# Query halves of the first two tiles ahead of the fused matrices in the head of an attention-branch backward kernel

## The chip, the cores and the metric

The kernel runs on one core of a Trainium2 chip. The metric is the device time of one execution in microseconds, as the median over runs. The engines are named as in the profile: PE is TensorE (PEld its weight loads), DVE is VectorE, ACT is ScalarE, POOL is GpSimd, and SP is SyncE, which only issues DMAs here.

## The reference

One block of a speech encoder is computed forward, then all gradients for a given output gradient. The forward part, cut:

```
xa = layernorm(x)                                  # x: 2 x 4000 x 144
q, k, v = split(xa @ w_qkv)
p = softmax(q @ k^T * 144**-0.5)                   # 4000 x 4000 for each batch
glob = (p @ v) @ w_att_out
h = gelu(layernorm(x) @ w_mlp_in)
u, g = split(h);  g = layernorm(g)
gc = depthwise_conv(g, dw_csgu, 5 taps over time)
loc = (u * gc) @ w_mlp_out
m = concat(glob, loc)
m = m + depthwise_conv(m, dw_merge, 5 taps over time)
out = x + m @ w_merge
```

The kernel returns `out` and the gradients of x and of the seven weights, in bf16.

## The kernel before, in words

The 4000 tokens of a batch are 32 blocks of 125. The two batches are worked off one after the other. For each, `phase_att` runs a loop over tiles t (one tile is one block of 125 queries) with eight steps s in each. A tile's work is spread over three turns of the loop:

- `S_pair(t, s)`, s = 0 to 3: two matmul pairs give 125x1000 scores in PSUM (L740, L741). DVE writes the running negative maximum (L745, L747), ACT the exponentials into `Pbuf` (L748).
- `rescale(t)` after s = 3: the four chunks are put on one maximum (L753, L757, L759), and SP issues the DMA that transposes all of P into `PT` (L760).
- One turn later `Y_half` (L768) multiplies `PT` by the normalized input, and `dP_pair` (L790, L791) makes the gradient of the scores, which DVE combines with P into `Sbuf` (L794). Later still `Z_half` (L810) and `X_group` (L849) use these.

`PT` exists once, and the PSUM pool for the scores and for dP has two buffers, which are handed out in the order of the program. All small products share a PSUM pool of three buffers.

A tile needs a query operand `qt` of two halves. The first half (for S) is the normalized input times the fused matrix `Q0` (and its last 16 rows in `RW`), Wq times Wk transposed. The second half (for dP) is the output gradient times the fused matrices `VUT` (and `RW`), which hold Wv, Wo, the taps of the depthwise convolution and w_merge in one. `jit_mm` (L707 to L714) and `jit_tr` (L722, L724) make both halves at once: a product into PSUM, two copies by ACT, PE transposes, one more copy. `jit_q` (L873 to L877), `jit_b` (L890 to L895) and `half_tr` (L884, L885) make one half each.

The head of the first batch is a program of its own (`head` in the main function). It loads x, the weights and the output gradient, and has these pieces:

- `st`, `mv`, `ln`, `xat` for each of four groups of eight blocks: statistics on DVE (L361 to L372), the power for the inverse deviation on POOL (L373), the factor on DVE (L377), normalizing of each block (L382 on ACT, L384 on DVE, L386 on POOL), PE transposes (L391, L395), and copies into `xaT_m` by ACT (L392) and into `R` by DVE (L396).
- `m1` makes `Q0`, `m1t` its transpose, `cols` the taps as columns, `taps` the products of w_merge with the taps (h = 0 on ACT, L217; h = 1 on POOL, L219), `tapr` their remainders on POOL (L223).
- `vo` makes the transposed weights WT; `vut` makes `VUT` from WT and the tap products (L232 to L239); `vu` makes what the output stage needs, and spills it to DRAM (small products on POOL, L261); `conv` makes the matrices of the local branch (POOL, L280 to L303, with ten tiny column loads).
- `gma`, `gm`, `gmb` transpose the output gradient into `goT` (L349, L350), `gs` its last 16 channels into `R` (L356, L357); `gr` copies these channels on POOL (L399).
- `clear` writes a block of zeros to DRAM (L1420, L1421), and `pads` loads these into the unused rows of `Pbuf` and `Sbuf` (L682, L683).

The order on the engines comes from the framework: it gives each instruction the priority of its place in the program and plans each engine's list ahead of time with its own estimates. An engine named in `manual_schedule` keeps the written order for the instructions traced inside; others may be put between them. Before the change this holds for POOL through the whole head (`k.head_order`) and for DVE in a block that ends ahead of the loop. The rest of the head is dealt out over the list `steps`: entry 8t + s is traced ahead of step s of tile t, for t = 0 and 1. From tile 2 on, `local_units` (the MLP branch) is dealt out over the loop; its tiles reuse the memory of the head's.

Of the kernel before, what the change touches and what calls it, by code (L numbers as in the profile page):

```python
# [14 lines left out]
D = 144  # L15
DR = 16
# [92 lines left out]
class Head:  # L109
# [7 lines left out]
    def loads(self):  # L117

        k, W, nc, wp, wt = self.k, self.W, self.k.nc, self.k.wpool, self.wt
        self.raw = wt.tile([128, 2, 7 * D], BF, name="raw")  # L120
        nc.vector.memset(self.raw[:, 1, :], 0.0)
        make_identity(nc, W.ident[:])
        self.two = wt.tile([128, 7, 2, D], BF, name="two")
        nc.gpsimd.memset(self.two[:, :, 1, :], 0.0)
        W.M1T = wp.tile([128, 2, D], BF, name="M1T")
        nc.gpsimd.memset(W.M1T[:, 1, :], 0.0)
        W.RW = wp.tile([128, 3 * D], BF, name="RW")
        nc.gpsimd.memset(W.RW[:], 0.0)
        W.Wi = wp.tile([128, 2, 2 * D], BF, name="Wi")
        nc.gpsimd.memset(W.Wi[:, 1, :], 0.0)  # L130
        self.Wi2 = wt.tile([DR, 2 * D], BF, name="Wi2")
        W.cols = wp.tile([128, 6, 5], F32, name="cols")
        nc.gpsimd.memset(W.cols[:], 0.0)
        self.dwt = wt.tile([5, 3 * D], BF, name="dwt")
        r = self.raw
        self.Wqkv, self.Wo, self.Wl = r[:, :, 0:3 * D], r[:, :, 3 * D:4 * D], r[:, :, 4 * D:5 * D]
        self.Wm = [r[:, :, (5 + h) * D:(6 + h) * D] for h in range(2)]

        def ld(t, ap, r0, eng=nc.scalar):
            eng.dma_start(t[0:128, 0, :], ap[r0:r0 + 128, :])  # L140
            eng.dma_start(t[0:DR, 1, :], ap[r0 + 128:r0 + D, :])
        ld(self.Wqkv, k.w_qkv, 0)
        ld(self.Wo, k.w_att_out, 0)
        nc.scalar.dma_start(self.dwt[:, 0:2 * D], k.dw_merge)
        nc.scalar.dma_start(self.dwt[:, 2 * D:3 * D], k.dw_csgu)
        ld(self.Wl, k.w_mlp_out, 0)
        for h in range(2):
            ld(self.Wm[h], k.w_merge, h * D, nc.sync)
        nc.scalar.dma_start(W.Wi[0:128, 0, :], k.w_mlp_in[0:128, :])
        nc.scalar.dma_start(W.Wi[96:96 + DR, 1, :], k.w_mlp_in[128:D, :])  # L150
        nc.scalar.dma_start(self.Wi2[:], k.w_mlp_in[128:D, :])

    def transp(self, src, c0, n):
        nc, ident = self.k.nc, self.W.ident
# [182 lines left out]
def pre_pieces(k, W, b, S, pst):  # L337
# [4 lines left out]
    if True:  # L342
        def v8(t, i0, n):
            return t[:, i0 * PB:(i0 + n) * PB].rearrange("p (a b) -> p a b", b=PB)

        def gomain(h0, n):
            pm = pst()
            for bi in range(n):
                nc.tensor.transpose(pm[:, bi, 0:PB], go_q[:, 2 + h0 + bi, 0:128], W.ident[0:PB, 0:PB])  # L349
            nc.scalar.copy(v8(S.goT, h0, n), pm[:, 0:n, 0:PB])  # L350

        def gostack(g):
            pm = pst()
            for bi in range(8):
                j = 8 * g + bi
                nc.tensor.transpose(pm[0:80, bi, 0:PB], S.go_r[:, j + 2:j + 7, :].rearrange("p a b -> p (a b)"), W.ident[0:PB, 0:PB])  # L356
            nc.vector.tensor_copy(v8(S.R, 8 * g, 8)[0:80], pm[0:80, :, 0:PB])  # L357

        def ln_st(g):
            for j in range(8 * g, 8 * g + 8):  # L360
                nc.vector.bn_stats(st[:, j, :], x_tp[:, j, :])  # L361

        def ln_mv(g):

            sl = slice(8 * g, 8 * g + 8)
            ma, mb, va, vb = st[:, sl, 1], st[:, sl, 4], st[:, sl, 2], st[:, sl, 5]
            nc.vector.tensor_tensor(S.dm[:, sl], ma, mb, op=ALU.subtract)
            nc.vector.tensor_tensor(S.sm[:, sl], ma, mb, op=ALU.add)
            nc.vector.tensor_tensor(veps[:, sl], va, vb, op=ALU.add)
            nc.vector.scalar_tensor_tensor(S.dm[:, sl], S.dm[:, sl], 0.25 * D, S.dm[:, sl], op0=ALU.mult, op1=ALU.mult)  # L370
            nc.vector.tensor_tensor(veps[:, sl], veps[:, sl], S.dm[:, sl], op=ALU.add)
            nc.vector.tensor_scalar(veps[:, sl], veps[:, sl], 1.0 / D, EPS, op0=ALU.mult, op1=ALU.add)  # L372
            nc.gpsimd.tensor_tensor(S.rstd_x[:, sl], veps[:, sl], k.mhalf[0:PB, sl], op=ALU.pow)  # L373

        def ln_nm(g):
            sl = slice(8 * g, 8 * g + 8)
            nc.vector.scalar_tensor_tensor(nmr[:, sl], S.sm[:, sl], -0.5, S.rstd_x[:, sl], op0=ALU.mult, op1=ALU.mult)  # L377

        def ln(g):
            for j in range(8 * g, 8 * g + 8):  # L380
                if S.act_ln and j % 2 == 0:
                    nc.scalar.activation(S.xa_aug[:, j, 0:D], x_tp[:, j, :], ACT.Identity, scale=S.rstd_x[:, j:j + 1], bias=nmr[:, j:j + 1])  # L382
                elif S.act_ln or j % 2:
                    nc.vector.tensor_scalar(S.xa_aug[:, j, 0:D], x_tp[:, j, :], S.rstd_x[:, j:j + 1], nmr[:, j:j + 1], op0=ALU.mult, op1=ALU.add)  # L384
                else:
                    nc.gpsimd.tensor_scalar(S.xa_aug[:, j, 0:D], x_tp[:, j, :], S.rstd_x[:, j:j + 1], nmr[:, j:j + 1], op0=ALU.mult, op1=ALU.add)  # L386

        def xat(g):
            pm = pst()
            for bi in range(8):  # L390
                nc.tensor.transpose(pm[:, bi, 0:PB], S.xa_aug[:, 8 * g + bi, 0:128], W.ident[0:PB, 0:PB])  # L391
            nc.scalar.copy(v8(S.xaT_m, 8 * g, 8), pm[:, :, 0:PB])  # L392
            pr = pst()
            for bi in range(8):
                nc.tensor.transpose(pr[0:112, bi, 0:PB], S.xa_aug[:, 8 * g + bi, 32:D], W.ident[0:PB, 0:PB])  # L395
            nc.vector.tensor_copy(v8(S.R, 8 * g, 8)[96:112], pr[96:112, :, 0:PB])  # L396

        def go_rem():
            nc.gpsimd.tensor_copy(S.go_r[:], go_q[:, :, 128:D])  # L399
        P = {}  # L400
        for g in range(G8):
            P["st%d" % g] = lambda g=g: ln_st(g)
            P["mv%d" % g] = lambda g=g: ln_mv(g)
            P["ln%d" % g] = lambda g=g: (ln_nm(g), ln(g))
            P["xat%d" % g] = lambda g=g: xat(g)
            P["gm%d" % g] = lambda g=g: gomain(2 + 8 * g, 8)
            P["gs%d" % g] = lambda g=g: gostack(g)
        P["gma"] = lambda: gomain(0, 2)
        P["gmb"] = lambda: gomain(NB + 2, 2)
        P["gr"] = go_rem  # L410
        return P
# [252 lines left out]
def phase_att(k, W, b, S, A, M, head=None):  # L664
# [6 lines left out]
    with ExitStack() as es:  # L671
# [225 lines left out]
        if head is None:  # L897
            jit_mm(0)
            jit_tr(0)
        else:  # L900
            steps = head(dict(pads=pads, clr=clr, jit_q=lambda: jit_q(0), jit_b=lambda: jit_b(0), jit_1=lambda: (jit_mm(1), jit_tr(1))))
        for t in range(NB + 1):
            xg = X_groups(t)
            if t == NB - 1:
# [7 lines left out]
            for s in range(8):  # L912
# [14 lines left out]
                        zt_tr(t - 3)  # L927
                    x(1)
                elif s == 1:
                    if ok(t + 1) and (t or head is None):  # L930
                        jit_mm(t + 1)
                    x(1)
                elif s in (2, 3):
# [2 lines left out]
                    if s == 3 and ok(t):  # L936
                        rescale(t)
                elif s == 4:
                    if ok(t + 1) and (t or head is None):
                        jit_tr(t + 1)  # L940
                    x(1)
                elif s == 5:
# [422 lines left out]
def kernel(ctx, tc, x, w_qkv, w_att_out, w_mlp_in, dw_csgu, w_mlp_out, dw_merge, w_merge, grad_out,  # L1365
# [61 lines left out]
    def head(f):  # L1427
# [5 lines left out]
        ones(S0)  # L1433
        pre_load_go(k, 0, S0, [nc.sync])
        f["clr"]()
        P = pre_pieces(k, W, 0, S0, lambda: k.ps_w.tile([128, 8, 128], BF, tag="w", name="pt"))

        k.head_order = ExitStack()
        k.head_order.enter_context(tc.manual_schedule(engines={nc.gpsimd.engine}))
        with tc.manual_schedule(engines={nc.vector.engine}):  # L1440
            for n in ("st0", "mv0", "st1", "mv1"):
                P[n]()
            hd.m1()
            hd.cols()
            P["ln0"]()
            hd.taps(1, 0, 4)
            for n in ("st2", "mv2", "xat0"):
                P[n]()
            f["jit_q"]()
            hd.vo()  # L1450
            P["ln1"]()
            hd.taps(1, 4, 8)
            for n in ("st3", "mv3", "xat1"):
                P[n]()
            hd.taps(0)
            P["ln2"]()
            hd.taps(1, 8, 10)
            hd.tapr(1)
            hd.tapr(0)
            P["xat2"]()  # L1460
            P["gr"]()
            P["ln3"]()
            clear()
            f["pads"]()
        steps = [[] for _ in range(16)]
        steps[0] = []
        steps[1] = [hd.m1t]
        steps[2] = [hd.vut]
        steps[3] = [P["xat3"], P["gs0"], P["gma"], P["gm0"]]
        steps[4] = [f["jit_b"], P["gs1"]]  # L1470
        steps[5] = [P["gm1"], f["jit_1"]]
        steps[6] = [P["gs2"], P["gm2"], lambda: hd.vu(0)]
        steps[9] = [P["gs3"], P["gm3"], P["gmb"], lambda: hd.vu(1)]
        steps[12] = [hd.conv, clear_a]
        steps[15] = [es_p0.close, k.head_order.close]
        return steps


# [109 lines left out]
```

## Time and profile before

| | |
|---|---|
| runs | 1464.2, 1464.32, 1468.26 us; median 1464.32 |
| profiled execution | 1460.56 us; span from first to last instruction 1458.8 us |
| mean granted clock of TensorE | 0.987 |
| busy share of the span | PE 94%, PEld 81%, DVE 81%, ACT 59%, POOL 20% |

The profiled execution is 3.8 us below the median. The head and the first tiles, in busy microseconds for each stretch of ten:

| stretch, us | PE | DVE | ACT | POOL | clock |
|---|---|---|---|---|---|
| 0 to 10 | 1.42 | 7.34 | 1.56 | 6.25 | 1.00 |
| 10 to 20 | 8.04 | 8.12 | 8.58 | 7.54 | 1.00 |
| 20 to 30 | 7.23 | 6.06 | 8.90 | 5.72 | 0.73 |
| 30 to 40 | 7.58 | 5.44 | 8.56 | 9.65 | 0.93 |
| 40 to 50 | 6.62 | 4.18 | 6.31 | 5.08 | 0.83 |
| 50 to 60 | 9.03 | 4.26 | 6.04 | 5.88 | 1.00 |
| 60 to 70 | 7.83 | 9.63 | 8.04 | 1.35 | 1.00 |
| 70 to 80 | 9.62 | 8.16 | 6.21 | 1.38 | 1.00 |

How to read a line in order of time: start, duration, engine, line of the kernel, operation, output<-inputs, shapes, how many were merged; in brackets, how long the engine had been idle and what ended that. Busy time of PE counts matmuls with modelled ends, so a busy PE isn't a PE at its peak. The clock column is the share of full speed that the throttle granted.

### The profile page before, as it was taken

The numbers are of one execution on the slowest core, as the hardware profiler recorded it, in microseconds if no ns is written. First come the engines' busy times: TensorE is split into PE (matmuls) and PEld (weight loads), VectorE is DVE, ScalarE is ACT, GpSimd is POOL, SyncE is SP. The second block draws the span as 40 slices with busy tenths as digits, with TensorE's granted clock in tenths as the row PEclk, the third lists the DMA queues.
The fourth block names the chain that finished last, engine by engine and source line by source line (L and its number), as shares of the span: only waits on it lengthen the run. The fifth ranks groups of instructions, "written<-read, shape, count | busy, mean of one in ns | idle before, by whom it ended". The sixth has DMA issues, their size and how long they took to land. (4 is left out here: it accounts for less than half of the span.)

```text
span 1458.8 us, 38954 instructions
## 1 busy us (share of the span) xinstructions
PE 1373.0 (94%) x16185; PEld 1180.9 (81%) x16185; DVE 1177.4 (81%) x2747; ACT 866.6 (59%) x1641; POOL 284.6 (20%) x507
## 2 busy tenths in 40 slices
PE   6799999999999999998887999999999999999798
PEld 4588888888888888887875888888888888888797
DVE  6699988888888888778458988888888888887754
ACT  6666666666666656524456665666666666554181
POOL 7411010111111110138312012111111111111420
PEclk9999999999999999999999999999999999999999
DMA  3576667666666766684226676666676666676712
GB/s 109 98 132 123 123 123 122 103 122 110 112 117 114 125 121 123 100 184 136 84 61 130 119 125 115 109 124 125 113 122 117 122 110 119 131 124 120 203 36 65
DMA packets 559390, 170.36 MB, mean 117 GB/s; under 512 B 542447, under 2 KB 554113, under 8 KB 559172
## 3 DMA queue, kind: packets, MB, share of 16 engines
q1 hardware_dynamic: 553370, 155.48, 57.8%
q0 software_dynamic: 5088, 12.11, 3.2%
q8 instruction: 126, 2.06, 0.6%
q14 instruction: 50, 0.41, 0.1%
q10 hardware_dynamic: 756, 0.30, 0.1%
HBM read 21.04 MB, written 14.12 MB: 24 GB/s over the span
## 5 line engine op out<-in xcount | busy, mean ns | idle before, releaser
L794 DVE SCALAR_TENSOR_TENSOR Sbuf<-ps,delta,Pbuf 125x1000 bf16<-125x1000 f32 x256 | 319.9, 1255 | 30.1 <-PE ps L791 28.1
L849 PE MATMUL X<-QBs,Sbuf 125*125 125x144 bf16 x2048 | 302.9, 226 | 6.5 <-DVE acc L855 2.7
L849 PE MATMUL X<-QBs,Pbuf 125*125 125x144 bf16 x2048 | 302.0, 226 | 0.0
L849 PEld LDWEIGHTS <-Pbuf 125*125 125x125 bf16 x2048 | 262.0, 137 | 15.2 <-issue 10.8
L849 PEld LDWEIGHTS <-Sbuf 125*125 125x125 bf16 x2048 | 261.8, 136 | 4.9
L855 DVE TENSOR_TENSOR acc<-X,acc 125x432 f32<-125x432 f32 x372 | 203.9, 551 | 32.9 <-PE X L849 32.0
L740 PE MATMUL ps<-xaT_m,qt 128*125 128x500 bf16 x512 | 193.6, 378 | 8.4 <-ACT Pbuf L748 6.3
L790 PE MATMUL ps<-xaT_m,qt 128*125 128x500 bf16 x512 | 191.8, 375 | 9.0 <-ACT Pbuf L748 5.9
L741 PE MATMUL ps<-R,qt 128*125 128x500 bf16 x512 | 192.7, 376 | 0.0
L791 PE MATMUL ps<-R,qt 128*125 128x500 bf16 x512 | 191.0, 373 | 0.0
L768 PEld LDWEIGHTS <-PT 125*125 125x125 bf16 x2048 | 148.5, 137 | 30.9 <-DMA PT<-Pbuf 12.8
L768 PE MATMUL yz<-xa_aug,PT 125*125 125x145 bf16 x2048 | 151.9, 228 | 10.5 <-DMA PT<-Pbuf 10.4
L810 PEld LDWEIGHTS <-ST 125*125 125x125 bf16 x1984 | 143.8, 137 | 16.9
L810 PE MATMUL yz<-xa_aug,ST 125*125 125x144 bf16 x1984 | 147.9, 227 | 0.0
L745 DVE TENSOR_SCALAR_CACHE_REDUCE Pbuf<-ps 125x1000 bf16<-125x1000 f32 x64 | 76.6, 1198 | 24.1 <-PE ps L741 23.5
L741 PEld LDWEIGHTS <-qt 128*125 128x125 bf16 x512 | 70.2, 137 | 30.0 <-issue 10.4
L791 PEld LDWEIGHTS <-qt 128*125 128x125 bf16 x512 | 69.5, 136 | 30.0 <-issue 9.5
L595 POOL TENSOR_TENSOR A_dwc<-l_fl,A_dwc 128x512 f32<-128x512 f32 (+2 forms) x48 | 35.7, 743 | 295.7 <-ACT l_fl L594 295.7
L790 PEld LDWEIGHTS <-qt 128*125 128x125 bf16 x512 | 69.8, 136 | 22.8 <-DVE Sbuf L794 2.1
L740 PEld LDWEIGHTS <-qt 128*125 128x125 bf16 x512 | 70.3, 137 | 20.4 <-ACT qt L724 0.6
L465 POOL TENSOR_SCALAR l_a<-l_sq 125x576 bf16<-125x576 bf16 x32 | 21.5, 670 | 298.1 <-ACT l_sq L463 245.2
L814 ACT ACTIVATE zn<-yz,rl 125x144 bf16<-125x144 f32 x64 | 24.1, 377 | 89.6 <-PE yz L810 88.9
(800 smaller groups left out, 3087.5 us busy)
## 6 DMA issues: line engine op xcount, KB each, us to landing
Yn_d<-yn SPq DMA_DIRECT2D x64, 35.2 KB
Zn_d<-zn SPq DMA_DIRECT2D x64, 35.2 KB
ug_d<-ugr SPq DMA_DIRECT2D x32, 70.3 KB
xo<-in_x_dram SPq DMA_DIRECT2D x16, 140.6 KB
out_dram<-dxo SPq DMA_DIRECT2D x16, 140.6 KB
go_h<-in_grad_out_dram POOLq DMA_DIRECT2D x4, 504.0 KB, 6.9
Zn<-Zn_d SPq DMA_DIRECT2D x4, 504.0 KB
PT<-Pbuf SPq DMA_TRANSPOSE x64
```

Of the source, the lines that this page charges most:

```text
L595: nc.gpsimd.tensor_tensor(acc, fl[0:rows, 0:n], acc, op=ALU.add)
L740: nc.tensor.matmul(ps[:, h, 0:CH], qt[:, 0, :], xaTm[:, cs], start=True, stop=False)
L741: nc.tensor.matmul(ps[:, h, 0:CH], qt[:, 1, :], R[:, cs], start=False, stop=True)
L745: nc.vector.tensor_scalar(pdst, src, -1.0, None, op0=ALU.mult, op1=ALU.min, accum_out=nm[:, 0:1])
L768: nc.tensor.matmul(Y, PT[0:PB, j, 0:PB], xaa[:, j, 0:D + 1], start=(j == 0), stop=(j == NB - 1))
L790: nc.tensor.matmul(ps[:, h, 0:CH], qt[:, 2, :], xaTm[:, cs], start=True, stop=False)
L791: nc.tensor.matmul(ps[:, h, 0:CH], qt[:, 3, :], R[:, cs], start=False, stop=True)
L794: nc.vector.scalar_tensor_tensor(sdst, ps[:, :, 0:CH].rearrange("p h (a b) -> p h a b", b=PB), DL[i][:], psrc, op0=ALU.subtract, op1=ALU.mult)
L810: nc.tensor.matmul(Z, ST[0:PB, j, 0:PB], xaa[:, j, 0:D], start=(j == 0), stop=(j == NB - 1))
L814: nc.scalar.activation(zn[:, 0:D], Z, ACT.Copy, scale=RL.pop(i)[:])
L849: nc.tensor.matmul(X[:, jj, :], l, r, start=(n_ == 0), stop=(n_ == len(ops) - 1))
L855: nc.vector.tensor_tensor(av, X[:, 0:nj, :], av, op=ALU.add)
```

## The change

Wi's three loads are issued by SP in place of ACT. In the first batch ACT normalizes two of eight blocks in place of four, POOL two, and DVE four as before. In the head's written block ACT keeps the written order too; `vo` is taken out of it, `jit_q(1)` comes in, and `xat3`, `taps(0)`, `tapr(0)`, `gr` and `pads` stand behind it. `clear` is traced ahead of the pieces. The query of tile 1 is made in two halves as that of tile 0 (`jit_q` early, `jit_b` at step 10), that of tile 2 whole at step 13, and the loop's own `jit_mm` and `jit_tr` begin with tile 2. The steps of the head's remaining pieces are new.

```diff
@@ -146,9 +146,9 @@
         ld(self.Wl, k.w_mlp_out, 0)
         for h in range(2):
             ld(self.Wm[h], k.w_merge, h * D, nc.sync)
-        nc.scalar.dma_start(W.Wi[0:128, 0, :], k.w_mlp_in[0:128, :])
-        nc.scalar.dma_start(W.Wi[96:96 + DR, 1, :], k.w_mlp_in[128:D, :])
-        nc.scalar.dma_start(self.Wi2[:], k.w_mlp_in[128:D, :])
+        nc.sync.dma_start(W.Wi[0:128, 0, :], k.w_mlp_in[0:128, :])
+        nc.sync.dma_start(W.Wi[96:96 + DR, 1, :], k.w_mlp_in[128:D, :])
+        nc.sync.dma_start(self.Wi2[:], k.w_mlp_in[128:D, :])
 
     def transp(self, src, c0, n):
         nc, ident = self.k.nc, self.W.ident
@@ -378,9 +378,9 @@
 
         def ln(g):
             for j in range(8 * g, 8 * g + 8):
-                if S.act_ln and j % 2 == 0:
+                if S.act_ln and j % 4 == 0:
                     nc.scalar.activation(S.xa_aug[:, j, 0:D], x_tp[:, j, :], ACT.Identity, scale=S.rstd_x[:, j:j + 1], bias=nmr[:, j:j + 1])
-                elif S.act_ln or j % 2:
+                elif j % 2:
                     nc.vector.tensor_scalar(S.xa_aug[:, j, 0:D], x_tp[:, j, :], S.rstd_x[:, j:j + 1], nmr[:, j:j + 1], op0=ALU.mult, op1=ALU.add)
                 else:
                     nc.gpsimd.tensor_scalar(S.xa_aug[:, j, 0:D], x_tp[:, j, :], S.rstd_x[:, j:j + 1], nmr[:, j:j + 1], op0=ALU.mult, op1=ALU.add)
@@ -898,7 +898,7 @@
             jit_mm(0)
             jit_tr(0)
         else:
-            steps = head(dict(pads=pads, clr=clr, jit_q=lambda: jit_q(0), jit_b=lambda: jit_b(0), jit_1=lambda: (jit_mm(1), jit_tr(1))))
+            steps = head(dict(pads=pads, clr=clr, jit_q=jit_q, jit_b=jit_b, jit=lambda i: (jit_mm(i), jit_tr(i))))
         for t in range(NB + 1):
             xg = X_groups(t)
             if t == NB - 1:
@@ -927,7 +927,7 @@
                         zt_tr(t - 3)
                     x(1)
                 elif s == 1:
-                    if ok(t + 1) and (t or head is None):
+                    if ok(t + 1) and (t > 1 or head is None):
                         jit_mm(t + 1)
                     x(1)
                 elif s in (2, 3):
@@ -936,7 +936,7 @@
                     if s == 3 and ok(t):
                         rescale(t)
                 elif s == 4:
-                    if ok(t + 1) and (t or head is None):
+                    if ok(t + 1) and (t > 1 or head is None):
                         jit_tr(t + 1)
                     x(1)
                 elif s == 5:
@@ -1433,46 +1433,48 @@
         ones(S0)
         pre_load_go(k, 0, S0, [nc.sync])
         f["clr"]()
+        clear()
         P = pre_pieces(k, W, 0, S0, lambda: k.ps_w.tile([128, 8, 128], BF, tag="w", name="pt"))
 
         k.head_order = ExitStack()
         k.head_order.enter_context(tc.manual_schedule(engines={nc.gpsimd.engine}))
-        with tc.manual_schedule(engines={nc.vector.engine}):
+        with tc.manual_schedule(engines={nc.vector.engine, nc.scalar.engine}):
             for n in ("st0", "mv0", "st1", "mv1"):
                 P[n]()
             hd.m1()
+            P["ln0"]()
             hd.cols()
-            P["ln0"]()
             hd.taps(1, 0, 4)
             for n in ("st2", "mv2", "xat0"):
                 P[n]()
-            f["jit_q"]()
-            hd.vo()
+            f["jit_q"](0)
             P["ln1"]()
             hd.taps(1, 4, 8)
             for n in ("st3", "mv3", "xat1"):
                 P[n]()
-            hd.taps(0)
+            f["jit_q"](1)
             P["ln2"]()
             hd.taps(1, 8, 10)
             hd.tapr(1)
-            hd.tapr(0)
             P["xat2"]()
-            P["gr"]()
             P["ln3"]()
-            clear()
-            f["pads"]()
+        P["xat3"]()
+        hd.taps(0)
+        hd.tapr(0)
+        P["gr"]()
+        f["pads"]()
         steps = [[] for _ in range(16)]
-        steps[0] = []
-        steps[1] = [hd.m1t]
-        steps[2] = [hd.vut]
-        steps[3] = [P["xat3"], P["gs0"], P["gma"], P["gm0"]]
-        steps[4] = [f["jit_b"], P["gs1"]]
-        steps[5] = [P["gm1"], f["jit_1"]]
-        steps[6] = [P["gs2"], P["gm2"], lambda: hd.vu(0)]
-        steps[9] = [P["gs3"], P["gm3"], P["gmb"], lambda: hd.vu(1)]
-        steps[12] = [hd.conv, clear_a]
-        steps[15] = [es_p0.close, k.head_order.close]
+        steps[2] = [hd.vo]
+        steps[4] = [hd.vut]
+        steps[5] = [P["gs0"], P["gma"], P["gm0"]]
+        steps[6] = [P["gs1"], P["gm1"]]
+        steps[7] = [hd.m1t]
+        steps[9] = [lambda: f["jit_b"](0), P["gs2"], P["gm2"]]
+        steps[10] = [lambda: f["jit_b"](1)]
+        steps[11] = [P["gs3"], P["gm3"], P["gmb"]]
+        steps[13] = [lambda: f["jit"](2)]
+        steps[14] = [lambda: hd.vu(0)]
+        steps[15] = [lambda: hd.vu(1), hd.conv, clear_a, es_p0.close, k.head_order.close]
         return steps
 
 
```

## The prediction

> **What bounds the kernel now.** I read the view of cores first (1458.8 us span, mean clock 0.987), then parts 1 and 2 of the page, then the busy times by stretch, and last each engine's instructions in order of time over the first 75 us, because every edit lies in the head: the steps before tile 2.
>
> ```profile
> 24.00:41.00 17.00, 12.14 (x117) 9.76 (x117) 9.06 (x20) 15.49 (x32) 13.72 (x43) 0.80 0.14 38
> 41.00:62.40 21.40, 17.47 (x144) 12.70 (x145) 10.82 (x19) 13.69 (x27) 10.03 (x25) 0.92 0.36 74
> 62.40:70.00 7.60, 6.01 (x55) 4.48 (x54) 7.23 (x11) 5.71 (x11) 1.35 (x2) 1.00 0.96 179
> 70.00:130.00 60.00, 57.39 (x606) 47.40 (x605) 53.01 (x112) 40.11 (x77) 7.34 (x15) 1.00 0.74 128
> 130.00:330.00 200.00, 196.22 (x2298) 168.31 (x2297) 174.03 (x378) 125.82 (x238) 26.10 (x41) 1.00 0.68 121
> ```
>
> The columns are stretch, length, busy time of PE, PEld, DVE, ACT, POOL, granted clock, DMA share, GB/s. From 130 us PE is busy 98% of the time at clock 1.00, so attention runs at PE's pace, and a head that ends earlier moves all that follows by as much. In the head PE isn't the bound: from 24 to 70 us it idles 4.86 + 3.93 + 1.59 = 10.4 us and loses 12.14 x 0.20 + 17.47 x 0.08 = 3.8 us to the lower clock. These 14.2 us are the most that the change can win there.
>
> ```profile
> 24.66 0.39 PE L391 MATMUL pt<-ident,xa_aug 125*128 125x125 bf16 x2 [1.23 <-ACT xa_aug L382]
> 33.20 0.69 DVE L396 COPY R<-pt 16x1000 bf16<-16x1000 bf16 x1 [1.67 <-PE pt L395]
> 36.09 1.26 DVE L747 TENSOR_SCALAR_CACHE_REDUCE Pbuf<-ps,nm__464 125x1000 bf16<-125x1000 f32 x1 [1.49 <-PE ps L741]
> 41.36 0.23 PE L722 MATMUL pt<-ident,qb 125*128 125x125 bf16 x1 [2.51 <-ACT qb L713]
> 45.56 1.20 DVE L745 TENSOR_SCALAR_CACHE_REDUCE Pbuf<-ps 125x1000 bf16<-125x1000 f32 x1 [2.30 <-PE ps L741]
> 50.73 1.23 PE L768 MATMUL yz<-xa_aug,PT 125*125 125x145 bf16 x16 [1.78 <-DMA PT<-Pbuf]
> 62.39 4.85 SPq L760 DMA_TRANSPOSE PT<-Pbuf  x1
> ```
>
> Here the reader sees three waits in a row. The transposed input of the last group of blocks is copied only at 33.2 us, so tile 0's last scores are reduced at 36.1. Tile 1's first scores come 9.5 us later (45.56), since its query (L713, L722) is made whole and so needs VUT and goT. Then tile 0's transposed P arrives (50.73). Tile 1's P goes out at 62.39.
>
> **Part by part.**
>
> *Wi's three loads, ACT to SP.* ACT loses two issues (0.43 + 0.44) before its first copy and the third (0.32 at 9.72), around which it stood from 8.29 to 10.08. The first fused product comes some 2.7 us earlier. It is worth nothing by itself: ln0 starts from VectorE's L377 at 9.79. SP issues the three (about 1.2 us) ahead of go_q, whose last load went out at 15.49; with one more stall as between 12.83 and 15.08 it is 19. GpSimd reads go_q at 24.60, which hides it; beyond 25 each us would delay the pads.
>
> *Normalizing.* ACT loses 8 of 16 pieces at a pitch of 0.42 (four took 1.69): 3.4 us. GpSimd gains 8. Their price is in the second batch:
>
> ```profile
> L386 POOL TENSOR_SCALAR xa_aug<-x_tp_n,rstd_x,lnnm x16: 453/540/1000, 684.1 to 695.8; 125x144 bf16<-125x144 bf16 x16
> ```
>
> Four together took 2.05 to 2.72 us, so two cost 1.0 to 1.4. They stand in GpSimd's written order behind the next group's power (L373, 1.65) and, from group 1 on, behind tap products (L219, 1.5 for four). GpSimd then runs: power 1 ends 11.6, ln0 12.8, taps 14.3, power 2 16.0, ln1 17.2, taps 18.7, power 3 20.5 (its input exists at 18.65), ln2 21.9, taps and tapr(1) 23.5, ln3 24.7.
>
> *ScalarE's order, vo out of the way.* Its two ln1 pieces follow the first qt (ends 16.68) at once, ending 17.6; now the last ends 19.7, behind vo. VectorE's list up to 18.65 is unchanged. Then, without its wait of 2.83: R of group 1 18.65 to 19.3 (now 21.49), ln2 to 20.6, one score reduction (1.20) to 21.8, R of group 2 from 22.6 (now 26.80), ln3 to 24.5. GpSimd's last piece (24.7), transposes (0.6 to 0.9) and R (0.69) put the last group at 26.3 instead of 33.89: **7.6 us earlier**. ACT between 10.9 and 26.3 must do cols 0.4, three xaT copies 2.9, two query halves 1.6, six pieces 2.5, two exponentials 2.1 and the ten tap products 3.6: 13.1 of 15.4 us. It fits, tightly.
>
> *Query halves first.* Tile 1's scores need jit_q(1) alone, so the 9.5 us gap after tile 0 goes. Next late is ACT's remaining work. It was busy 15.49 + 13.69 = 29.2 us from 24 to 62.4. Off go eight pieces 3.4, one xaT copy 1.0, two exponentials 2.1 and the last tap 0.4; vo's copies (1.2) come on: 23.5 us from 26.5. How densely ACT can run is unknown. It ran 76% over 24 to 62.4 and 91% over 24 to 41, where no transposed P was awaited. I take the middle, 83.5%, since one such wait (41.10 to 50.73) stays: 23.5 / 0.835 = 28.1, so tile 1's P goes out at 54.7 instead of 62.4, **7.7 us**. The ends are 57.4 (5.0) and 52.3 (10.1). The two gains are one: the first is contained in the second.
>
> *Zeros and pads earlier.* The memset and the store of zdram (0.25 + 0.80) fit into GpSimd's wait of 2.20 before 7.42. Off its later list come these and 2.38 of waiting. With ln, tapr(0) and go_r (0.8 + 0.7) its pads start at 26 instead of 28.93, so the list behind them ends near 53.7 instead of 56.7:
>
> ```profile
> 55.53 1.19 POOL L434 MEMSET gd<- 32x576 bf16 x2
> 65.31 0.67 POOL L465 TENSOR_SCALAR l_a<-l_sq 125x576 bf16<-125x576 bf16 x1 [8.58 <-issue]
> ```
>
> The first local unit would want GpSimd at 65.3 - 7.7 = 57.6: covered by 3.9 us. Past a gain of 11.6 that cover is gone and GpSimd is the next bound.
>
> *Moved matrices.* vo, vut, m1t, jit_b, vu and conv keep their instructions and DMAs; vu's spills and conv's column loads stay on SP and GpSimd. Behind jit_b's eviction on ACT stand tile 1's exponentials, and for them wait DMA and PE.
>
> Sum: 7.7 us off the profiled execution's 1460.6 gives 1452.9; the runs' median stands 3.8 higher (1464.3), so off the median it is **1456.6**. A measurement of this kernel tells about 0.3% (4.4 us) from no change.
>
> **The clock.** PE's clock was 0.50 from 25 to 30 us, with PE busy 4.22 of those 5 us, and 0.67 from 40 to 45; the longest wait of PE from 12 to 30 us was 1.23 us. [...]
>
> **The rivals.**
>
> 1. *All packs.* The idle and the lower clock go as far as GpSimd's list allows: 11.6 off, **1453**. For it: 14.2 us are there. Against: tile 0's transposed P still takes 7 to 9.6 us from issue to use (62.39 to 69.34; 41.10 to 50.73).
>
> 2. *The wait moves to jit_b.* dP of tile 0 needs VUT (0.37 + 1.76), the first goT copies (0.42 + 0.99 + 0.99) and jit_b (0.83) on ACT: 5.4 us that ran during tile 0 now stand after it. If PE stands there in its order, 7.7 - 5.4 = 2.3 is left: **1462**. It is also what is left if the framework's order doesn't bring tile 1's scores forward. Against: ACT has from 30 us to about 40 for it, until the transposed P is there.
>
> 3. *GpSimd is held by VectorE.* Beside four L384 (687.44 to 688.45) two of its pieces took 0.47 each; beside L1160, with two SBUF inputs, 0.92 and 1.00. If the head's pieces took 1.0, the list above grows by 1.0 per group, 4 in all: **1461**. In the head VectorE then runs statistics and one-input pieces, which speaks against it. [...]
>
> 4. *Slower: the clock stays at half.* From 26 us PE has about 22 us of full-clock work until tile 1's P is out. Each us of it at half clock costs one more. From 7.7 on the gain is gone, from 12 (24 us of time at half) the kernel is slower by over 4.4; at 0.5 for 28 us, 14 extra, it is 6 slower: **1470**. For it: 0.50 and 0.67 above, in stretches with many short transposes. Against: both were over within 5 us (0.86 and 0.99 in the next).
>
> **How the numbers follow.** Forecast 0.47, rival 1 0.15, rival 2 0.21, rival 3 0.07, rival 4 0.10. The forecast's own range is 1454 to 1459.5. Faster by over 0.3% (below 1459.9): 0.45 + 0.15 + 0.02 = 0.62. Within: 0.02 + 0.20 + 0.05 = 0.27. Slower: 0.10 + 0.01 = 0.11. From 1450 (all of the 14.2 us) to 1466 only rival 4 and some hundredths at the two ends are left out.
>
> **What would show it.** Right: the last L396 copy of R near 26 us; tile 1's first L745 within 3 us of tile 0's last L747; its transposed P issued near 55 us; ACT busier than 80% from 26 on; PE 98% busy from 130 us as now. Wrong: a PE wait on jit_b ahead of L790 or on GpSimd's pieces ahead of L391 (rivals 2, 3), a clock under 0.7 for over 10 us (4), or local units waiting for GpSimd or for the spills of the head's last tiles, so that what is won by 55 us is given back by 100 us.

## The result and the profile after

| | before | after |
|---|---|---|
| median (lowest to highest), us | 1464.32 (1460.11 to 1469.37) | 1455.59 (1452.24 to 1458.45) |
| runs | 7 | 7 |
| profiled execution; its span, us | 1460.56; 1458.8 | 1457.65; 1455.9 |
| mean granted clock | 0.987 | 0.990 |

The changed kernel is 8.7 us faster between the medians; 1456.6 us had been forecast. The measured ratio of the two is 0.9929, interval 0.9911 to 0.9947, which is 7.8 to 13.0 us. The two profiled executions differ by 2.9 us only. So the head has to be looked at by itself, and for that this text uses a **lead**: by how many microseconds a tile's P goes out to be transposed (L760) earlier than the same tile's in the profile of before shown above. From tile 6 to the end of the first batch the lead is the same for every tile within 0.3 us.

The same five stretches of the changed kernel (start:end, length, busy time of PE, PEld, DVE, ACT, POOL with instructions, granted clock, DMA share, GB/s):

```profile
24.00:41.00 17.00, 13.37 (x119) 9.48 (x117) 9.40 (x19) 13.23 (x29) 14.38 (x46) 0.90 0.45 95
41.00:62.40 21.40, 18.70 (x170) 13.78 (x170) 15.51 (x24) 14.85 (x33) 11.27 (x25) 1.00 0.38 79
62.40:70.00 7.60, 7.53 (x79) 6.16 (x78) 6.79 (x13) 7.37 (x15) 1.77 (x3) 1.00 0.76 142
70.00:130.00 60.00, 56.90 (x634) 48.02 (x633) 54.35 (x115) 39.92 (x76) 8.68 (x17) 1.00 0.75 133
130.00:330.00 200.00, 196.21 (x2278) 167.85 (x2276) 171.99 (x374) 126.35 (x238) 25.06 (x39) 1.00 0.66 118
```

From 130 us nothing has changed: PE 98% busy, as before. Ahead of it PE's idle time fell from 4.86 + 3.93 + 1.59 us to 3.63 + 2.70 + 0.07 us, and the time lost to the lower clock from 3.8 to 13.37 x 0.10 = 1.3 us. The instructions that answer to the waits shown of before, in order of time within each engine:

```profile
12.95 0.39 PE L391 MATMUL pt<-ident,xa_aug 125*128 125x125 bf16 x2 [1.94 <-POOL xa_aug L386]
20.51 0.69 DVE L396 COPY R<-pt 16x1000 bf16<-16x1000 bf16 x1 [1.01 <-PE pt L395]
28.54 0.69 DVE L396 COPY R<-pt 16x1000 bf16<-16x1000 bf16 x1
31.18 1.26 DVE L747 TENSOR_SCALAR_CACHE_REDUCE Pbuf<-ps,nm__472 125x1000 bf16<-125x1000 f32 x1 [1.95 <-PE ps L741]
40.20 1.20 DVE L745 TENSOR_SCALAR_CACHE_REDUCE Pbuf<-ps 125x1000 bf16<-125x1000 f32 x1 [1.75 <-PE ps L741]
51.86 4.87 SPq L760 DMA_TRANSPOSE PT<-Pbuf  x1
71.39 5.34 SPq L760 DMA_TRANSPOSE PT<-Pbuf  x1
53.02 0.23 PE L722 MATMUL pt<-ident,qb 125*128 125x125 bf16 x1 [1.57 <-ACT qb L713]
52.78 1.19 POOL L434 MEMSET gd<- 32x576 bf16 x2
64.69 0.67 POOL L465 TENSOR_SCALAR l_a<-l_sq 125x576 bf16<-125x576 bf16 x1 [10.72 <-PE ps L741]
```

The last copy of R comes at 28.54 (33.20 before), tile 0's last reduction at 31.18 (36.09), tile 1's first at 40.20 (45.56). Tile 1's P goes out at 51.86 instead of 62.39, a lead of 10.5 us. But tile 2's goes out at 71.39 instead of 76.13, a lead of 4.7, and 5.5 is what stays. Half of what had been won by 52 us is gone 20 us later. Against the second profile of before (below), in which tile 1's P goes out at 63.99, it is 12.1 us first and 6.9 us in the end: 5 us are given back there too. GpSimd's list ends at 53.97 and its next work comes 10.7 us after that, so it isn't what takes it. These are the stretches between tile 1's and tile 2's P, first of the kernel before, then of the changed one, with the columns of above:

```profile
62.39:76.13 13.74, 12.15 (x110) 9.23 (x109) 11.93 (x25) 10.64 (x19) 1.77 (x3) 1.00 0.84 156
```

```profile
51.86:71.39 19.53, 18.30 (x168) 14.20 (x169) 16.28 (x28) 14.92 (x33) 3.83 (x7) 1.00 0.68 137
```

Between the same two events PE now has 168 matmuls instead of 110, and is 94% busy with them. Tile 1's P overtook other work of PE, and that work didn't come earlier by as much: when P goes out, the trace holds 293 matmuls so far, 335 before. The 42 that were passed over still have to be done.

### The profile page after: what moved, and what is told of

Same layout as the page of the kernel before. It is cut to its first block, busy times and chain, and to the rows that moved or that the text cites. A ratio compares the mean times of both kernels' runs of the same rounds, so it can differ in the third digit from the quotient of the medians.

```text
span 1455.9 us, 38963 instructions
## 1 busy us (share of the span) xinstructions
PE 1371.7 (94%) x16186; PEld 1180.2 (81%) x16186; DVE 1179.7 (81%) x2747; ACT 863.0 (59%) x1636; POOL 289.0 (20%) x515
## 3 DMA queue, kind: packets, MB, share of 16 engines
HBM read 21.04 MB, written 14.12 MB: 24 GB/s over the span
## 5 line engine op out<-in xcount | busy, mean ns | idle before, releaser
L849 PEld LDWEIGHTS <-Pbuf 125*125 125x125 bf16 x2048 | 262.0, 137 | 15.2 <-issue 10.8
L740 PE MATMUL ps<-xaT_m,qt 128*125 128x500 bf16 x512 | 193.2, 377 | 9.9 <-ACT Pbuf L748 6.7
L790 PE MATMUL ps<-xaT_m,qt 128*125 128x500 bf16 x512 | 191.8, 375 | 9.1 <-ACT Pbuf L748 6.1
L741 PE MATMUL ps<-R,qt 128*125 128x500 bf16 x512 | 192.3, 376 | 0.6 <-DVE R L357 0.4
L768 PEld LDWEIGHTS <-PT 125*125 125x125 bf16 x2048 | 149.2, 138 | 28.2 <-DMA PT<-Pbuf 10.1
L741 PEld LDWEIGHTS <-qt 128*125 128x125 bf16 x512 | 70.4, 137 | 28.7 <-issue 9.2
L740 PEld LDWEIGHTS <-qt 128*125 128x125 bf16 x512 | 70.2, 137 | 22.2 <-issue 1.8
L790 PEld LDWEIGHTS <-qt 128*125 128x125 bf16 x512 | 69.7, 136 | 22.7 <-DVE Sbuf L794 2.1
```

Of the source, the lines that this page charges most:

```text
L740: nc.tensor.matmul(ps[:, h, 0:CH], qt[:, 0, :], xaTm[:, cs], start=True, stop=False)
L741: nc.tensor.matmul(ps[:, h, 0:CH], qt[:, 1, :], R[:, cs], start=False, stop=True)
L768: nc.tensor.matmul(Y, PT[0:PB, j, 0:PB], xaa[:, j, 0:D + 1], start=(j == 0), stop=(j == NB - 1))
L790: nc.tensor.matmul(ps[:, h, 0:CH], qt[:, 2, :], xaTm[:, cs], start=True, stop=False)
L849: nc.tensor.matmul(X[:, jj, :], l, r, start=(n_ == 0), stop=(n_ == len(ops) - 1))
```

## The experiments

Two readings stood against each other. One is the prediction's: tile 1's query halves bring what lasts. The other: their lead is given back as soon as PE is the bound, and what lasts is what PE wins in idle time and lower clock in the whole head, most of it by the chain of the input (normalize, transpose, copy into R). Each expectation says what it calls the theory and the rival. "Lead" in the expectations is the lead just defined, in the steady part of the first batch. The kernel before had a median of 1465 to 1467 us beside these runs. Each experiment is an edit of the changed kernel where nothing else is said. The lead of each comes from one profile.

### The changed kernel again, and the kernel before again

`after_again` and `before_again` are unchanged.

> The changed kernel once more, to see what of its gain is the head's. In the first pair of profiles tile 1's P goes out 10.5 us earlier, but from tile 4 of the first batch on the lead is a steady 5.5 us. Theory A (only TensorE's recovered idle time and clock last; the rest of tile 1's lead has no TensorE work behind it): the steady lead is again 5 to 6 us, and a total gain of more than that comes from elsewhere, above all between the batches, and scatters. Theory B (the forecast's: the lead of tile 1's P lasts): the steady lead of another execution is 8 to 10 us and the first profile was an odd one. Total against before: 6 to 10 us less under both.

> The kernel before once more, for its profile: whether its first profile, at 1460.56 us below its median, had an unusually early head. Theory: the head is the same within 0.5 us (tile 1's P at 62.4, tile 6's at 148.5), and the execution differs between and behind the batches. Rival: the head itself comes later in a typical execution, and the lead of 5.4 us is too low for that reason.

Measured: after again 1457.15 us, ratio 0.9953 (0.9938 to 0.9969), lead 5.35; P of tiles 0 to 2 at 35.49, 52.06, 71.60. Before again, one execution: 1466.2 us, lead -1.42; P at 40.82, 63.99, 77.78. The lead of the changed kernel repeats within 0.2 us, that of the kernel before within 1.4, where I had expected 0.5.

### Tile 1 whole again

```diff
-            f["jit_q"](1)
...
-        steps[7] = [hd.m1t]
+        steps[7] = [hd.m1t, lambda: f["jit"](1)]
...
-        steps[10] = [lambda: f["jit_b"](1)]
```

> Undoes one part: tile 1's query is made whole again, once the fused matrices and the first transposes of the output gradient are there (same step as M1T), all else as changed. Theory: the early halves of tile 1 are the main part, since without them TensorE and VectorE wait for VUT between tile 0's last scores and tile 1's first. Then tile 1's first reduction comes some 3 to 5 us later than in the changed kernel (40.2 us there), and 2 to 4 us of the steady lead of 5.5 are lost. Rival: the gain is that of the input chain (the last copy into R 4.7 us earlier), because in the changed kernel tile 1's first scores already stand behind the transposes of the output gradient (L741 at 38.36); then less than 1 us is lost.

Measured: 1457.73 us, ratio 0.9955 (0.9940 to 0.9969), lead 6.92. In order of time:

```profile
41.93 1.20 DVE L745 TENSOR_SCALAR_CACHE_REDUCE Pbuf<-ps 125x1000 bf16<-125x1000 f32 x1 [4.17 <-PE ps L741]
53.16 4.91 SPq L760 DMA_TRANSPOSE PT<-Pbuf  x1
```

VectorE does wait 4.17 us for tile 1's scores, and its P goes out 1.1 to 1.3 us later than in the two profiles of the changed kernel. Yet nothing is lost: the ratio is that of the changed kernel on the same chip (0.9953), and the lead is 1.4 to 1.6 larger, since the clock stayed at 1.00 from 24 to 41 us (0.90 there). Of the two cases in the expectation it is the one in which less than 1 us is lost. By idle time alone, without the clock, the two are level (9.2 us here and 9.5 and 9.4 in the changed kernel, table below). Undoing the part that I had built the gain on costs nothing.

### The halves alone, on the kernel before

```diff
-            f["jit_q"]()
+            f["jit_q"](0)
...
+            f["jit_q"](1)
...
-        steps[4] = [f["jit_b"], P["gs1"]]
-        steps[5] = [P["gm1"], f["jit_1"]]
+        steps[4] = [lambda: f["jit_b"](0), P["gs1"]]
+        steps[5] = [P["gm1"]]
...
+        steps[10] = [lambda: f["jit_b"](1)]
+        steps[13] = [lambda: f["jit"](2)]
```

> One part done alone, on the kernel before: the query halves of tiles 0 and 1 early (tile 1's after the transposes of group 1), the other half of tile 1 at step 10 and tile 2's query at step 13, as in the change; loads, normalizing, ScalarE's planning and all other steps as before. Theory now (the lead that lasts is idle time and half clock taken from TensorE in the input chain, tile 1's query has no part in it): last copy into R stays near 33, steady lead under 1.5 us, total within 0.2% of before. Rival (the forecast's): tile 1's first reduction comes some 5 us earlier than 45.6 and 3 us or more of it last.

Measured: 1468.19 us, ratio 1.0005 (0.9993 to 1.0017), lead -4.71.

```profile
41.71 1.19 DVE L745 TENSOR_SCALAR_CACHE_REDUCE Pbuf<-ps 125x1000 bf16<-125x1000 f32 x1
59.20 1.26 DVE L747 TENSOR_SCALAR_CACHE_REDUCE Pbuf<-ps,nm__698 125x1000 bf16<-125x1000 f32 x1 [1.62 <-PE ps L741]
50.54 4.16 PE L768 MATMUL yz<-xa_aug,PT 125*125 125x145 bf16 x32 [4.05 <-DMA PT<-Pbuf]
```

Tile 1's first scores come 3.9 us earlier (45.56 before), its last ones don't: they stand behind tile 0's products with PT, for which PE waits 4.05 us. P goes out at 64.12, not earlier than 62.39. The total is the one expected, while the lead is lower than I had thought: of the 4.7 us, 3.0 are the clock's and about 2 idle time (table below). The halves alone are worth nothing.

### ScalarE's order, normalizing and vo put back, one at a time

```diff
-        with tc.manual_schedule(engines={nc.vector.engine, nc.scalar.engine}):
+        with tc.manual_schedule(engines={nc.vector.engine}):
```

> Undoes one part: in the head's written block ScalarE is planned by the framework again, VectorE and GpSimd keep the written order. Theory: the input chain was sped up by taking vo out of it, so the order itself is worth little: last copy into R within 1 us of 28.5, steady lead 4.5 to 6. Rival: without the order the products of w_merge and the exponentials get in front of the normalizing pieces, the last copy comes 2 us or more later and 2 us or more of the lead are lost.

```diff
-                if S.act_ln and j % 4 == 0:
+                if S.act_ln and j % 2 == 0:
```

> Undoes one part: ScalarE normalizes four of eight blocks again and GpSimd none. Theory: GpSimd's pieces (two took 0.90 to 0.95 us in the head) are bound to the slow chain of powers and tap products, and ScalarE had waits of 2.4 and 0.8 us around its own pieces, so the move is worth 0 to 1 us either way. Rival (the forecast's working): 3.4 us of ScalarE work come back into a tightly filled stretch, so the last copy into R comes 1.5 us or more later and as much of the lead is lost.

```diff
             f["jit_q"](0)
+            hd.vo()
...
-        steps[2] = [hd.vo]
```

> Undoes one part: vo stands again in the written block, behind tile 0's query half, ahead of group 1's pieces, now in ScalarE's written order as well; all else as changed. Theory: vo's copies and the products between them hold ScalarE ahead of group 1's pieces, the last copy into R comes 1.5 to 3 us later than 28.5, and 1 to 3 us of the steady lead of 5.4 are lost. Rival: ScalarE had waits of 2.4 and 0.8 us in this stretch, vo fits into them, VUT comes earlier and the lead stays or grows.

| | median, us | ratio | lead | last copy of R |
|---|---|---|---|---|
| act_free | 1459.59 | 0.9964 (0.9951 to 0.9977) | 3.08 | 30.18 |
| ln_on_act | 1460.07 | 0.9974 (0.9958 to 0.9990) | 2.48 | 29.03 |
| vo_back | 1461.79 | 0.9964 (0.9951 to 0.9977) | 3.16 | 31.57 |

Each costs 2.2 to 2.9 us of the lead of 5.35, though the last copy of R moves by only 0.5 to 3.0 us. With vo back, VectorE waits for its transposes, and with four pieces on ACT too; first the one, then the other:

```profile
31.57 0.69 DVE L396 COPY R<-pt 16x1000 bf16<-16x1000 bf16 x1 [2.73 <-PE pt L395]
```

```profile
29.03 0.69 DVE L396 COPY R<-pt 16x1000 bf16<-16x1000 bf16 x1 [1.17 <-PE pt L395]
```

Where ACT's order is free, the loss is the clock's, here in stretches of 5 us:

```profile
25.00:30.00 5.00, 4.55 (x33) 3.57 (x30) 3.73 (x10) 3.12 (x5) 4.17 (x16) 0.50 0.28 96
30.00:35.00 5.00, 4.60 (x39) 3.08 (x37) 1.96 (x3) 4.05 (x11) 5.00 (x13) 0.97 0.18 30
35.00:40.00 5.00, 3.50 (x32) 3.12 (x32) 1.60 (x3) 3.83 (x9) 4.86 (x20) 0.72 0.41 76
```

At 0.50 PE is 4.55 us busy. In the kernel before, L740 and L741 followed each other every 0.42 us at 0.50 (28.36 to 29.61) and every 0.21 at 1.00 (35.04 to 35.68); by that the 4.55 us would be about 2.3 at full clock, an estimate. So each of the three parts is worth some of the lead in its profile, but not in the same way. In PE's idle time (table below; 9.5 and 9.4 in the changed kernel) `vo_back` loses 1.7 us, `ln_on_act` 0.7 and `act_free` nothing. The clock takes 1.3 us more than in the changed kernel in `ln_on_act` and 2.9 in `act_free`, and one profile each doesn't show that this part belongs to the edit and not to the one execution. The totals don't settle it, for all three intervals overlap that of the changed kernel (0.9938 to 0.9969). My expectations for `act_free` (4.5 to 6 us of lead left) and for `ln_on_act` (0 to 1 us lost) were too good. That the short pieces of `ln_on_act` keep ACT from copies that PE waits for is a guess that fits, not shown.

### The output gradient's transposes moved out of tile 1's way

In the changed kernel tile 1's first L741 (38.36) stands behind 34 transposes of the output gradient (35.41 to 38.4, from 36.2 on at half clock: eight took 0.60 us at 35.41 and 1.05 at 36.68). Here they are traced later:

```diff
-        steps[6] = [P["gs1"], P["gm1"]]
...
-        steps[9] = [lambda: f["jit_b"](0), P["gs2"], P["gm2"]]
+        steps[9] = [lambda: f["jit_b"](0)]
...
-        steps[11] = [P["gs3"], P["gm3"], P["gmb"]]
+        steps[11] = [P["gs1"], P["gm1"]]
+        steps[12] = [P["gs2"], P["gm2"]]
...
-        steps[14] = [lambda: hd.vu(0)]
+        steps[14] = [P["gs3"], P["gm3"], P["gmb"], lambda: hd.vu(0)]
```

> An attempt at a better version, and a test: the transposes of the output gradient that only tile 2 and later need (gs1 to gs3, gm1 to gm3, gmb) go from steps 6, 9 and 11 to 11, 12 and 14. In the changed kernel tile 1's first scores stand in TensorE's list behind those of step 6 (33.63 to 38.36). Theory (TensorE's work bounds what lasts): tile 1's first reduction comes 2 to 4 us earlier than 40.2, but at most 1 us of that is left at tile 6. Rival (forecast): most of these 2 to 4 us last.

Measured: 1455.95 us, ratio 0.9934 (0.9919 to 0.9949), lead 7.89.

```profile
37.85 1.20 DVE L745 TENSOR_SCALAR_CACHE_REDUCE Pbuf<-ps 125x1000 bf16<-125x1000 f32 x1 [1.17 <-PE ps L741]
49.01 4.87 SPq L760 DMA_TRANSPOSE PT<-Pbuf  x1
```

Tile 1's scores come 2.35 us earlier and the steady lead is 2.5 larger, where I had expected that 1 us at most would last. 1.3 of the 2.5 is the half clock, which doesn't occur here from 24 us on; most of the rest is PE's idle time (8.6 us instead of 9.5). `late_whole` is this kernel with tile 1 whole:

> The version with the later transposes, with tile 1's query made whole at the step of M1T. Theory (tile 1's early halves have no part in what lasts, TensorE's idle time and clock from 24 to 130 us have): steady lead 7 to 8 us, as without this edit (7.9). Rival: with the transposes out of the way the early halves are what lets tile 1's scores start, so 1.5 us or more of the lead are lost.

Measured: 1457.78 us, ratio 0.9946 (0.9927 to 0.9965), lead 4.35.

```profile
42.69 1.20 DVE L745 TENSOR_SCALAR_CACHE_REDUCE Pbuf<-ps 125x1000 bf16<-125x1000 f32 x1 [6.17 <-PE ps L741]
```

Here my expectation (a lead of 7 to 8 us) failed and the rival of that text holds: with the transposes out of the way the halves are worth 3.5 us of lead. 2.55 of it is the clock (0.60 and 0.72 from 35 to 45 us), in one profile; 0.7 is PE's idle time. The intervals of the two ratios overlap.

### Eighteen unused matmuls

```diff
+        def warm(n):
+            pw = k.ps_yz.tile([PB, 2, 145], F32, tag="yz", name="warm")
+            for _ in range(n):
+                nc.tensor.matmul(pw..., W.ident[:, 0:PB], wz[:], start=True, stop=True)
...
+            warm(18)
             f["jit_q"](0)
```

`wz` holds the constant 0.5; nobody reads what these matmuls write. `warm` is the changed kernel with them, `warm_late` the one with the later transposes, `warm_before` the kernel before.

> The changed kernel with 18 extra matmuls of a constant in TensorE's waits up to tile 0's query (8, 6 and 4 of them; nobody reads their result), to see what half clock costs in the input chain. In the changed kernel the 1000-column groups of transposes up to 20 us go at 0.105 us each and those after 23 us at 0.055, and VectorE waits 1.04 and 1.01 us for the first two groups. Theory: with TensorE at full clock by 15 us the second copy into R (20.5) comes 0.5 to 1 us earlier and the steady lead grows by 0.5 to 1.5 us. Rival: the chain goes by VectorE, ScalarE and GpSimd alone, or the clock is not raised by so few; the lead stays within 0.3 us of 5.4, or falls by the extra matmuls' time.

> The same extra matmuls on the version with the later transposes of the output gradient (steady lead 7.9 us, full clock from 24 us on). Theory: as there, 0.5 to 1.5 us more than 7.9, the best of all. Rival: no more than 7.9.

> The kernel before with the same 18 extra matmuls (10, 5, 1 and 2 of them in TensorE's waits up to tile 0's query), nothing of the change. Theory: what lasts is TensorE's idle time and half clock, and half clock costs the kernel before 3.8 to 4 us from 24 to 62 us (clock 0.80 and 0.92, and 0.90 and 0.84 in its second profile). If the early full clock carried through, the steady lead would be 2 to 5 us and the total 0.15 to 0.35% less, about half of the change's gain without any of its edits. Rival: half clock returns in the waits that the kernel before keeps (2.5 us on tile 1's query, then on the transposed P), so the lead stays under 1.5 us.

| | median (range), us | ratio | lead |
|---|---|---|---|
| warm | 1453.16 (1449.22 to 1455.87) | 0.9914 (0.9897 to 0.9931) | 9.64 |
| warm_late | 1455.08 | 0.9924 (0.9909 to 0.9940) | 9.15 |
| warm_before | 1464.58 | 0.9993 (0.9983 to 1.0004) | 0.38 |

`warm` in stretches, then in order of time:

```profile
24.00:41.00 17.00, 14.01 (x139) 9.95 (x139) 9.89 (x20) 14.28 (x31) 16.18 (x50) 1.00 0.43 79
41.00:62.40 21.40, 19.45 (x183) 14.80 (x182) 15.73 (x23) 15.37 (x34) 9.01 (x22) 1.00 0.58 117
62.40:70.00 7.60, 7.45 (x79) 6.15 (x79) 7.46 (x20) 5.56 (x11) 1.82 (x3) 1.00 0.27 51
70.00:130.00 60.00, 57.60 (x635) 48.46 (x635) 54.56 (x117) 40.22 (x78) 8.64 (x17) 1.00 0.77 140
```

```profile
16.90 0.39 PE L391 MATMUL pt<-ident,xa_aug 125*128 125x125 bf16 x4
26.75 0.69 DVE L396 COPY R<-pt 16x1000 bf16<-16x1000 bf16 x1
48.27 4.91 SPq L760 DMA_TRANSPOSE PT<-Pbuf  x1
```

Four transposes take 0.39 us at 16.90. In the changed kernel they take longer:

```profile
18.58 0.63 PE L391 MATMUL pt<-ident,xa_aug 125*128 125x125 bf16 x4
```

In the changed kernel the clock's first record is at 22.5 us, and four transposes take 0.39 us at 26.76. The last copy of R comes 1.8 us earlier in `warm`, and no half clock follows (1.00 in all four stretches). I had expected 0.5 to 1.5 us more lead; it is 4.3 more, 2.0 of them idle time and 1.3 clock from 24 us on. `warm_late` gained 1.3 on the version without the matmuls, as expected, though the clock took 1.4 us there from 24 us on (table below); the best of all, as I had expected, it is not. On the kernel before the same matmuls bring nothing that shows, and there the clock falls back:

```profile
20.00:25.00 5.00, 4.55 (x25) 3.00 (x24) 2.42 (x7) 3.82 (x11) 3.64 (x11) 0.50 0.24 85
```

`warm` has the lowest median of all. Its ratio lies below that of the second set of runs of the changed kernel (0.9953) with intervals apart; with that of the first (0.9929) the intervals overlap.

### The sum that holds for all fourteen profiles

For each profile: PE's idle time from 24 to 130 us, and its busy time there times what the clock lacks, stretch by stretch as above. What is less of both than in the first profile of before should be the lead. This is close to bookkeeping: where PE is the bound behind 130 us and its work is the same, the lead must be what PE lost less. So the table says where the lead lies, and not which edit made it.

| kernel | idle | clock | less than before | lead |
|---|---|---|---|---|
| before; again | 13.0; 13.0 | 3.8; 4.0 | 0; -0.2 | 0; -1.4 |
| after; again | 9.5; 9.4 | 1.3; 1.3 | 6.0; 6.1 | 5.5; 5.35 |
| tile1_whole | 9.2 | 0 | 7.6 | 6.9 |
| halves_alone | 15.2 | 6.8 | -5.2 | -4.7 |
| act_free | 9.1 | 4.2 | 3.5 | 3.1 |
| ln_on_act | 10.1 | 2.7 | 4.0 | 2.5 |
| vo_back | 11.2 | 1.3 | 4.4 | 3.2 |
| late_go | 8.6 | 0 | 8.2 | 7.9 |
| late_whole | 9.3 | 2.55 | 5.0 | 4.35 |
| warm | 7.5 | 0 | 9.3 | 9.6 |
| warm_late | 6.6 | 1.4 | 8.8 | 9.15 |
| warm_before | 11.7 | 3.4 | 1.8 | 0.4 |

The two columns agree within 1.6 us everywhere. When tile 1's P goes out doesn't: in `vo_back` it has a lead of 9.4 and keeps 3.2. The reading by PE's idle time and clock holds; the one by tile 1's P falls. How much of the clock column belongs to a kernel and how much to the one execution is open: a single stretch of 3.4 us at half clock makes 1.3 us of it in both profiles of the changed kernel.

**What stays open** is the rest of the time. The gain between medians is larger than the lead in every one of these kernels, mostly by 2 to 4 us (after 8.7 against 5.5, after again 8.3 against 5.35, `warm` 13.6 against 9.6). By the ratios it is less sure: the intervals of six of the twelve take the lead in. It would follow if the execution first profiled of before, 3.8 us below the median, had a head some 3 us better than usual; the second profile of it has one 1.4 us worse. And the stretch from the last P of the first batch to tile 4's of the second takes 198.3 us in the one and 203.2 in the other profile of the same kernel before, 201.1 and 200.9 in the two of the changed one, 199.2 in `warm`, 204.8 in `tile1_whole`. That scatter of 5 us is as large as the lead. No run here takes it apart, and single executions can't be compared by their totals for it.

## Why the prediction was right, and where it was not

**PE as the bound from 130 us, and 14.2 us as the most**: right. 98% and clock 1.00 in all profiles of that stretch, and no kernel got a larger lead than 9.6.

**Wi's three loads**: right. The first fused product came 2.8 us earlier (its copy by ACT, L184, at 8.29 instead of 11.12), and ln0 still waited for VectorE's L377 (9.86; 9.79 before).

**Normalizing**: two pieces took 0.89 to 0.95 us, below my 1.0 to 1.4. Behind the second power, as written, ln0's ended at 13.37 (I had 12.8), and PE waited 1.94 for them; the first copy of R came at 14.64 (14.12 before).

**ScalarE's order, vo out**: right in kind, 4.7 us instead of 7.6. I had let VectorE go on without a wait once its 2.83 was gone. It waited 1.04 and 1.01 us for transposes that ran at half clock, as their pitch shows (0.63 us for four, later 0.39). It took two score reductions between the copies of groups 1 and 2 instead of one, and a third ahead of the last copy.

**Query halves first**: this is the step that failed. I had 7.7 us for tile 1's P and took it to last to the end. P came even earlier, 10.5 us, though ACT was busy only 76% of the time (21.67 of 28.40 us from 26.3 on, where I took 83.5%). The other term was off the other way: ACT had 19.5 us of work from 26.3 us until P went out, not 23.5, since the copies of vu, conv and the third tile's query (some 4 us) now come behind it. But half of the lead was given back by tile 2, since PE had 42 matmuls fewer behind it and became the bound at once. Undone, the halves cost nothing (0.9955 against 0.9953); alone, they bring nothing (1.0005). Only with the later transposes was lead lost without them, most of it by the clock. The 9.5 us gap after tile 0 didn't go either: tile 1's first reduction still comes 9.0 us after tile 0's last one (31.18 to 40.20), behind vut and the transposes of the output gradient. I named the sign of this, "given back by 100 us", but looked for it at GpSimd and the spills.

**Zeros and pads**: the store of zdram was issued behind the second power (11.63, not before 7.42) and the pads started at 28.49 instead of 26. The end of GpSimd's list is right: 53.97, forecast 53.7, with 10.7 us of cover.

**Rivals.** All packs (1453): not reached by the change; `warm` reached 1453.16. The wait moves to jit_b: ahead of L790 there is none, and 1.57 us at 53.02 for the third tile's query. GpSimd held by VectorE: no, a piece took 0.44 to 0.50 us, as beside L384 in the second batch (0.47). The clock stays at half: half clock does come back (0.66 from 35 to 40 us in the changed kernel), its size is 1.3 us instead of 14. The most that I gave, 14.2 us, was counted from 24 us on; half clock ahead of that, which the clock column doesn't show, was not in it.

So the number was right for a reason that is right in part. The pieces of the head had the right sign and place, but the input chain's lead was 4.7 us instead of 7.6, and that of tile 1's P didn't last: 5.5 us stayed, not 7.7. Some 3 us that I can't place came on top, and that the two errors cancel is luck. Measured from the second profile of before the lead is 6.9 us, so part of the gap may lie in the profile that I started from.

## What to carry to other kernels

A lead at one event lasts only as far as the engine that bounds the rest has less idle time behind it: add up that engine's idle time and its loss to the clock over the whole head, and don't follow a single wait. A part that removes the most visible wait can be worth nothing, while work taken out of the way far ahead of it on another engine is worth something (vo, 1.7 us of PE's idle time). Look at the clock of every edit: 2.5 of the 6.0 us that PE lost less are clock, so a single profile can mislead by a fall more or less. The eighteen unused matmuls brought 4.3 us of lead in `warm`, where the clock then stayed at 1.00, 1.3 in `warm_late`, where the clock took 1.4 us, and on the kernel before (0.4) nothing that shows.

## What the runs showed of the hardware

The clock fell without a long wait. These are 5 us stretches of the changed kernel, and PE's two waits ahead of the fall:

```profile
30.00:35.00 5.00, 3.59 (x32) 2.54 (x33) 2.18 (x4) 3.85 (x11) 5.00 (x13) 1.00 0.19 30
35.00:40.00 5.00, 4.59 (x42) 3.70 (x41) 1.36 (x2) 3.65 (x9) 4.61 (x21) 0.66 0.82 152
40.00:45.00 5.00, 4.09 (x40) 2.74 (x39) 3.80 (x6) 3.83 (x8) 4.98 (x11) 1.00 0.36 61
```

```profile
33.63 0.37 PE L740 MATMUL ps<-xaT_m,qt 128*125 128x500 bf16 x1 [0.65 <-ACT Pbuf L748]
35.41 0.60 PE L356 MATMUL pt<-ident,go_r 125*80 125x125 bf16 x8 [0.90 <-ACT VUT L239]
```

The waits are 0.65 and 0.90 us. In the kernel before the clock was 0.50 from 25 to 30 us, and PE's longest wait from 12 to 30 us was 1.23; its next fall, at 41.68, came right behind the wait of 2.51. In `halves_alone` it was 0.81 from 45 to 50 us and 0.51 from 50 to 55; by the 0.81 it fell at about 48.1, some 1.6 us after the wait of 4.05 shown above had begun. So there are falls without a long wait and falls with one.

The busy time of a stretch of 5 us doesn't tell it either. From 30 to 35 us PE was busy 3.59 us in the changed kernel, and the clock fell in the next stretch. It was busy less in `tile1_whole` and `warm`, and the clock stayed at 1.00 in the next two (first the one, then the other):

```profile
30.00:35.00 5.00, 2.87 (x29) 2.17 (x29) 2.17 (x4) 3.88 (x10) 5.00 (x13) 1.00 0.20 30
35.00:40.00 5.00, 3.69 (x50) 3.17 (x50) 1.36 (x2) 4.00 (x10) 4.59 (x21) 1.00 0.85 158
40.00:45.00 5.00, 4.41 (x54) 3.52 (x51) 3.03 (x6) 3.28 (x7) 4.88 (x11) 1.00 0.32 55
```

```profile
30.00:35.00 5.00, 3.17 (x41) 2.48 (x39) 2.22 (x5) 4.66 (x11) 5.00 (x16) 1.00 0.18 29
35.00:40.00 5.00, 4.80 (x56) 3.57 (x55) 3.52 (x6) 4.23 (x9) 4.59 (x19) 1.00 1.07 199
40.00:45.00 5.00, 4.07 (x35) 2.81 (x34) 3.05 (x5) 4.32 (x8) 3.68 (x9) 1.00 0.03 0
```

So neither one wait nor the busy time of 5 us says in these runs when the clock falls; that stays open.

The granted clock in the stretches is 1.00 for the changed kernel from 10 to 20 us, though four transposes take 0.63 us at 18.58 and 0.39 at 26.76. L740 and L741 follow each other every 0.42 us from 20.50 to 21.34, as at the recorded 0.50 in the kernel before, and every 0.21 from 25.95 to 26.37. The clock's first record is at 22.52 us there and at 21.20 in the kernel before. So ahead of its first record the column doesn't show the half clock, and the pitch of equal matmuls does: the 1.00 in the first two rows of the table of before isn't a measured full clock.
